# A fourth silu buffer, a reordered unit end, a cast moved by one step and two deferred stores in a fused attention and SwiGLU kernel

## The chip, the cores and the metric

The kernel runs on one core of a Trainium2 chip. The core has five engines with one instruction queue each: TensorE (PE in the profile; its weight loads are shown apart, as PEld), VectorE (DVE), ScalarE (ACT), GpSimd (POOL) and SyncE (SP), which here only issues DMAs. Each engine runs its instructions in the order in which the program issues them and waits on semaphores for the others. The metric is the time of one execution on the device in microseconds; lower is better.

## The reference

Two stages, in float32. Linear attention with a decay per head works on 64-row blocks with a running state `kv_state`; its output, reshaped to 3072 tokens of 512 columns, goes through a SwiGLU block.

```python
# q, k, v: (4, 8, 768, 64); lam: one decay per head
for b in range(nb):
    sl = slice(b * block, (b + 1) * block)
    qb, kb, vb = (q[:, :, sl].copy(), k[:, :, sl].copy(), v[:, :, sl].copy())
    intra = np.einsum('bhic,bhjc->bhij', qb, kb) * Dmask[None]
    intra = np.einsum('bhij,bhjd->bhid', intra, vb)
    inter = np.einsum('bhid,bhde->bhie', qb * lam_pow[None], kv_state)
    out[:, :, sl] = intra + inter
    kb_dec = kb * rev_pow[None]
    kv_state = lam_block[None, :, None, None] * kv_state + np.einsum('bhsd,bhse->bhde', kb_dec, vb)
...
x = np.ascontiguousarray(attn_out.transpose(0, 2, 1, 3)).reshape(B * S, H * D)   # (3072, 512)
g = x @ w_gate                         # w_gate, w_val: (512, 1536)
silu = g * (1.0 / (1.0 + np.exp(-g)))
return (silu * (x @ w_val) @ w_out)    # w_out: (1536, 512)
```

## The kernel before

**Groups and tiles.** The sequence is cut into blocks of 128 rows. A group is two consecutive blocks of one batch element with all 8 heads; there are 12 groups. A tile is two groups, 512 tokens; there are 6 tiles (0 to 5). Attention is done group by group and writes, transposed and in bf16, into the tile's `xt`; the SwiGLU block is done tile by tile. The attention of later groups is woven between the matmuls of earlier tiles.

**Attention of a group.** SP loads k, q and v as float32 (`load_group`). `cast_scaled` (line 285) makes the bf16 tile `qk`: ACT casts k (line 289), DVE, or POOL if so told, scales q (line 291), and then `dma_transpose` (line 276) lets SP issue one transposing DMA into `qkt`. `v_scale` (line 263) makes `v_s` on POOL. On PE follow `scores` (lines 358 or 388; DVE masks them into `ssb`, lines 365 or 393), `upd_mm` (line 420, the update of the state; ACT copies it out, as `kvn` at line 434 and `ups` at line 442, and POOL sums it up in `state`), and the two halves of the output in one pair of banks: `intra` (line 527, from `ssb` and `v_s`) and `inter` (line 514, from `qkt` and the state). Between those two, `guard` (line 498) is a one-column ACT copy out of the output bank; the second half on PE waits for it. `evac` (line 540 or 543) copies the result into `xt`. For group 2, `upd_core` (line 905) issues it in the order: update, first copy, intra, guard, inter, evac, second copy. The queries of groups 0 to 2, which PE transposes, are scaled by the table `qdec` (line 326); the other groups don't read it.

**SwiGLU of tiles 0 to 3.** `ffn_gate` and `ffn_val` (lines 573 and 588) do one 128-column piece of the hidden width: four matmuls for the gate, ACT's silu into a buffer `sil` (line 586), four matmuls for the value, and a DVE product into `h` (line 603). PSUM has eight banks, handed out in turn. Pieces are `steps`; a table `plan`, filled with `at(step, function, ...)`, says what else is issued behind each step, in the order of the `at` calls. Steps of tile 0 are `s0[2]` to `s0[10]`, `s0["11a"]` and `s0["11b"]`; the last two each work on one group.

**SwiGLU of tiles 4 and 5: units.** Here each block product is done with seven block matmuls in place of eight. `ffn_unit` (line 712) is one of three units of a tile. Its operands are sums of blocks of `xt`, of the weights and, for the output, of `h`, made on DVE by `x_combo`, `w_combo` and `h_combo` (lines 710, 692, 666). These sums wait in a list, `trickle`; `drip(n)` issues the next n of them. A unit makes four pairs of silu (ACT, line 756) and product (line 759). The products are on DVE but for the second, which is on POOL. `dr[2]` is the number of sums issued at the unit's end; it is 2 or 3. `mid`, in the first two units of tile 4, issues the first half of the attention of groups 10 and 11.

**Output.** `out_units` (line 801) does the output matmul of tiles 1 to 5 with seven products (line 819), `p1` to `p7`, copies into a buffer `osb`, and stores on SP. For tile 1 it is done in two calls, one per group of the tile; the second call (`t=1, gs=(1,)`) is completed by `out_rest` behind step 9 of tile 2. Its two stores (256 KB each) stand on SP behind the loads of group 9.

**Order on SP around the deferred stores.** Behind step 8 of tile 2: transposition of group 8, loads of group 9. Behind step 9: the two stores. Behind step 0 of tile 3: transposition of group 9, loads of group 10. Behind step 6: transposition of group 10, loads of group 11.

**Buffers.** `sil` has 3 buffers, `h` 5, `osb` 4. A buffer is given out again, in program order, to a later tile of the same tag; the first instruction that writes it waits for the last reader of the one before.

The end of a unit, as it is now:

```python
        for i in range(2):
            product(i, E[i], wa(1, 1), xsum(2))
        silu((1, 0), E[0])
        mult(nc.vector, 1, 0, E[1])
        drip(dr[2])
        if mid:
            mid()
        for i in range(2):
            product(i, Bb[i], wsum(2), xb(1, 1))
        silu((0, 1), Bb[0])
        mult(nc.vector, 0, 1, Bb[1])
        h_combo(t, j)
```

Of the kernel before, what the change touches and what calls it, by code (L numbers as in the profile page):

```python
# [9 lines left out]
BF16 = mybir.dt.bfloat16  # L10
# [27 lines left out]
def _body(ctx, tc, nc, q, k, v, lam, moe_w_gate, moe_w_val, moe_w_out, out):  # L38
    B, H, S, D = q.shape
    HP = H // 2  # L40
# [28 lines left out]
    ssb_pool = ctx.enter_context(tc.tile_pool(name="ssb", bufs=2))  # L69
    xt_pool = ctx.enter_context(tc.tile_pool(name="xt", bufs=2))  # L70
    h_pool = ctx.enter_context(tc.tile_pool(name="h", bufs=5))
    sil_pool = ctx.enter_context(tc.tile_pool(name="sil", bufs=3))
    osb_pool = ctx.enter_context(tc.tile_pool(name="osb", bufs=4))
    kv_pool = ctx.enter_context(tc.tile_pool(name="kv", bufs=1))
    psum = ctx.enter_context(tc.tile_pool(name="psum", bufs=1, space=bass.MemoryType.PSUM))
# [121 lines left out]
    dec = const.tile([128, H, 8], FP32, name="dec")  # L197
    qdn = const.tile([128, H, 2], FP32, name="qdn")
    lamgrp = const.tile([128, HP], FP32, name="lamgrp")
    qdec = const.tile([128, HP, 2, 2 * M], BF16, name="qdec")  # L200
    nc.scalar.activation(ln_lam, lam_ps[:, 0:H], AF.Ln)
    for h2 in range(2):
        nc.scalar.activation(lnp[h2 * 64:h2 * 64 + 64, :],
# [72 lines left out]
    def dma_transpose(g):  # L276
        t = st[("qk", g)]
        tt = qkt_pool.tile([128, 2, 2, HP, 128], BF16, name="qkt", tag="qkt")
        nc.sync.dma_start(out=tt.rearrange("p a s h n -> p (a s h) n"),
                          in_=t.rearrange("p a s x -> p (a s x)"), transpose=True)  # L280
        st[("qkt", g)] = tt

    QP = ()

# [46 lines left out]


    KACT = ()
    later = []

    def run_later(n):
# [314 lines left out]
    def h_combo(t, j, g=None):  # L651


        fs = slice(0, FH) if g is not None else slice(2 * j[0], 2 * j[1]) if type(j) is tuple else slice(2 * j, 2 * j + 2)
        g0, g1 = (0, B // 2) if g is None else (g, g + 1)
        ha, hb = st[("h", t, 0)], st[("h", t, 1)]
        a11, a21 = ha[:, fs, 2 * g0:2 * g1:2], ha[:, fs, 2 * g0 + 1:2 * g1:2]
        a12, a22 = hb[:, fs, 2 * g0:2 * g1:2], hb[:, fs, 2 * g0 + 1:2 * g1:2]
        for i in range(3):
            if ("hs", t, i) not in st:  # L660
                st[("hs", t, i)] = raw_pool.tile([128, FH, B // 2, BLK], BF16, name="hs", tag="raw")
        s = [st[("hs", t, i)][:, fs, g0:g1] for i in range(3)]
        for o, i0, i1, op in ((s[0], a21, a22, ALU.add), (a21, a11, a21, ALU.subtract),
                              (s[1], s[0], a11, ALU.subtract), (s[2], a12, s[1], ALU.subtract)):
            trickle.append((t, lambda o=o, i0=i0, i1=i1, op=op:
                            nc.vector.tensor_tensor(out=o, in0=i0, in1=i1, op=op)))
# [3 lines left out]
    def drip(n):  # L670
        for _ in range(min(n, len(trickle))):
            trickle.pop(0)[1]()
# [39 lines left out]
    def ffn_unit(t, j, bk, early=None, mid=None, dr=(0, 0, 2)):  # L712


        xt = st[("xt", t)]
        for half in range(2):
            if ("h", t, half) not in st:
                st[("h", t, half)] = h_pool.tile([128, FH, B, BLK], BF16, name="h", tag="h")
        hs2 = [st[("h", t, half)][:, 2 * j:2 * j + 2] for half in range(2)]
        A, E, Bb = [[banks[k] for k in bk[2 * m:2 * m + 2]] for m in range(3)]  # L720
        for k in bk:
            primed[k] = 512
        es = [kv_pool.tile([128, 2 * HP * D], FP32, name="es", tag="ups", bufs=4) for _ in range(2)]
        sil = {}

        def product(i, o, lhs, rhs, start=False):
            for fi in range(2):
                for c in range(KH):
                    nc.tensor.matmul(o[:, fi * 256:fi * 256 + 256], lhs(i, c, 2 * j + fi), rhs(c),  # L729
                                     start=(start and fi == 0 and c == 0), stop=(c == KH - 1),  # L730
                                     skip_group_check=True)

        def wa(k, half):
            def f(i, c, fc):
                f0 = (FH * half + fc) * 128
                return (wg_sb, wv_sb)[i][:, KH * k + c, f0:f0 + 128]
            return f

        def wsum(n):
            return lambda i, c, fc: ws[i, n][:, c, fc * 128:fc * 128 + 128]  # L740

        def xb(k, r):
            return lambda c: xt[:, :, KH * k + c, r]

        def xsum(n):
            return lambda c: xs[t][:, n, :, c]

        def h_of(half, r):
            return hs2[half][:, :, r:B:2]

        def v3(x):
            return x.rearrange("p (f g n) -> p f g n", f=2, g=2)

        def silu(key, src):
            sil[key] = sil_pool.tile([128, 512], BF16, name="sil", tag="sil")
            nc.scalar.activation(sil[key], src, AF.Silu)  # L756

        def mult(eng, half, r, src):
            eng.tensor_tensor(out=h_of(half, r), in0=v3(sil[half, r]), in1=v3(src), op=ALU.mult)  # L759

        for i in range(2):
            product(i, A[i], wa(0, 0), xb(0, 0), True)
            nc.scalar.copy(out=Bb[i], in_=A[i])
        for i in range(2):
            product(i, E[i], wa(0, 1), xb(0, 1), True)
            nc.scalar.copy(out=es[i], in_=E[i])
        if early:
            early()
        for i in range(2):
            product(i, Bb[i], wsum(1), xsum(1))  # L770
            nc.vector.tensor_tensor(out=E[i], in0=Bb[i], in1=es[i], op=ALU.add)  # L771
        run_later(len(later))
        drip(dr[0])
        for i in range(2):
            product(i, A[i], wa(1, 0), xb(1, 0))
        silu((0, 0), A[0])
        for i in range(2):
            product(i, Bb[i], wsum(0), xsum(0))
            nc.vector.tensor_tensor(out=es[i], in0=Bb[i], in1=es[i], op=ALU.add)
        mult(nc.vector, 0, 0, A[1])  # L780
        silu((1, 1), es[0])
        mult(nc.gpsimd, 1, 1, es[1])
        drip(dr[1])
        for i in range(2):
            product(i, E[i], wa(1, 1), xsum(2))
        silu((1, 0), E[0])
        mult(nc.vector, 1, 0, E[1])
        drip(dr[2])
        if mid:
            mid()  # L790
        for i in range(2):
            product(i, Bb[i], wsum(2), xb(1, 1))
        silu((0, 1), Bb[0])
        mult(nc.vector, 0, 1, Bb[1])
        h_combo(t, j)

    def out_row(t, b):
# [3 lines left out]
    def out_units(t, gs=(0, 1), last=False, n=7, bk=None, many=None):  # L801
# [20 lines left out]
        def store(g, r, c0, c1, eng=nc.sync if t >= SY else nc.scalar):  # L822
            b = groups[2 * t + g]
            row = b[0] * S + (b[1] * 2 + r) * BLK
            eng.dma_start(out=bass.AP(tensor=out.tensor, offset=out.offset + row * DM + c0,
                                      ap=[[DM, 128], [1, c1 - c0]]), in_=O[g][r][:, c0:c1])

        def p1(g):
            product(A[g], lambda f: ha[:, f, 2 * g], lambda f: wo_sb[:, f, 0:HD], True)
# [203 lines left out]
    def at(n, fn, *a):  # L1033
        plan.setdefault(n, []).append((fn, a))
# [22 lines left out]
    at(s0[9], scores, 2)  # L1057
    at(s0[9], run_later, 4)
    at(s0["11a"], upd_core, 2, SPLIT)
    at(s0[10], cast_scaled, 3, nc.gpsimd)  # L1060
    at(s0[10], load_group, 4, "v")
    at(s0["11b"], v_scale, 3, nc.gpsimd)
    at(s0["11b"], state, 2)
    at(s0["11b"], load_group, 5, "kq")
# [219 lines left out]
```

## Time and profile before

| | us |
|---|---|
| three timed runs: median (lowest to highest) | 218.67 (218.20 to 220.88) |
| profiled execution, its time | 217.92 |
| profiled execution, span from first to last instruction | 216.2 |
| DVE busy in the span | 147.6 |
| ACT busy in the span | 130.6 |

The granted TensorE clock is 1.000 over the whole span. HBM reads are 28.31 MB and writes 6.29 MB.

How rows are read. A timeline row gives the start in us from the span's start, the duration, the engine, the line, the operation, the tile written and the tile read, the shape, and in brackets how long the engine stood idle before it and what it waited for; `x4` is four such instructions in a row, and the duration then is that of all. The suffix q marks an engine's queue where it issues DMAs. A row of waits gives engine, line and tile of who waited, then whom it waited for, the total in us, the number of times and the longest. A row of a tile's view gives shortest, median and longest duration in ns. Matmuls are pipelined, so their rows overlap.

### The profile page before, as it was taken

How to read it: one execution, taken by the hardware profiler on the slowest of the kernel's cores; microseconds unless marked ns; L12 is line 12 of the kernel's file. 1: busy time of each engine (PE TensorE's matmuls, PEld its weight loads, DVE VectorE, ACT ScalarE, POOL GpSimd, SP SyncE). 2: the span in 40 equal slices, each digit the busy share in tenths (PEclk: the TensorE clock that was granted, in tenths of full speed). 3: DMA queues.
4: the chain of work that ended last, by engine and by line, in shares of the span. 5: the costliest groups of instructions: out<-in, count | busy, mean ns of one | idle time of the engine just before them, and what ended most of it. 6: DMA issues, size and time to landing. Idle time of an engine off the chain costs nothing.

```text
span 216.2 us, 6854 instructions
## 1 busy us (share of the span) xinstructions
PE 209.1 (97%) x2797; PEld 153.9 (71%) x2801; DVE 147.6 (68%) x267; ACT 130.6 (60%) x280; POOL 92.1 (43%) x128
## 2 busy tenths in 40 slices
PE   8889999899999999999999999999999999999993
PEld 3566455788888448856754545888888888888882
DVE  1774347576687889765478967887798389961750
ACT  6888576666536154548378587774882676636522
POOL 6685755828499140686953145140730022200200
PEclk9999999999999999999999999999999999999999
DMA  6999999999996788899789859763000500005014
GB/s 193 343 355 382 374 326 293 295 245 232 375 315 137 193 223 199 223 160 256 199 207 222 203 116 212 179 171 126 2 5 3 194 0 3 0 3 194 0 52 147
DMA packets 82177, 39.77 MB, mean 184 GB/s; under 512 B 45410, under 2 KB 77794, under 8 KB 82146
## 3 DMA queue, kind: packets, MB, share of 16 engines
q1 hardware_dynamic: 80946, 38.74, 65.3%
q10 hardware_dynamic: 1200, 0.59, 0.9%
q8 instruction: 22, 0.36, 0.7%
q14 instruction: 9, 0.07, 0.1%
HBM read 28.31 MB, written 6.29 MB: 160 GB/s over the span
## 4 chain that ended last, share of the span: by engine, by line
PE 89%; ACT 3%; DVE 3%; issue 1%; POOLq 1%; POOL 1%; DVEq 0%
PE bank L819 21%; PE bank L581 19%; PE bank L599 19%; PE bank L729 15%; PE bank L619 5%; PE bank L527 2%; PE bank L514 2%; DVE ssb L365 2%; PE bank L420 1%; PE bank L358 1%; PE bank L320 1%; PE bank L388 1%; PE bank L188 1%; ACT sil L756 1%; PE bank L154 1%
## 5 line engine op out<-in xcount | busy, mean ns | idle before, releaser
L603 DVE TENSOR_TENSOR h<-sil,bank 128x256 bf16<-128x256 bf16 (+1 forms) x67 | 35.1, 533 | 29.1 <-PE bank L599 17.6
L581 PE MATMUL bank<-xt,wg_sb 128*128 128x256 bf16 (+1 forms) x276 | 52.6, 315 | 0.0
L599 PE MATMUL bank<-xt,wv_sb 128*128 128x256 bf16 (+1 forms) x276 | 52.4, 314 | 0.0
L586 ACT ACTIVATE sil<-bank 128x256 bf16<-128x256 f32 (+1 forms) x67 | 31.8, 480 | 22.6 <-PE bank L581 17.6
L599 PEld LDWEIGHTS <-wv_sb 128*128 128x128 bf16 x276 | 26.9, 98 | 14.7 <-POOL wv_sb L249 0.2
L581 PEld LDWEIGHTS <-wg_sb 128*128 128x128 bf16 x276 | 26.0, 98 | 13.3 <-DVE xt L540 0.2
L266 POOL TENSOR_TENSOR v_s<-v,dec 128x512 bf16<-128x512 f32 (+1 forms) x18 | 23.2, 1308 | 25.4 <-DMA v<-in_v_dram 21.4
L759 POOL TENSOR_TENSOR h<-sil,es 128x512 bf16<-128x512 bf16 x6 | 7.0, 1167 | 47.9 <-ACT sil L756 47.9
L819 PEld LDWEIGHTS <-h 128*128 128x128 bf16 x240 | 23.3, 98 | 3.6 <-issue 0.6
L819 PE MATMUL bank<-wo_sb,h 128*128 128x256 bf16 x180 | 21.6, 273 | 0.1
L819 PEld LDWEIGHTS <-hs 128*128 128x128 bf16 x180 | 17.6, 98 | 2.7
L365 DVE TENSOR_TENSOR ssb<-bank,causal 128x512 bf16<-128x512 f32 x24 | 15.4, 683 | 2.0 <-PE bank L358 2.0
L729 PEld LDWEIGHTS <-ws 128*128 128x128 bf16 x144 | 13.8, 97 | 2.3 <-issue 0.2
L475 POOL TENSOR_TENSOR kvf<-kvs,ups 128x256 f32<-128x256 f32 x8 | 6.5, 815 | 20.5 <-ACT ups L442 20.5
L771 DVE TENSOR_TENSOR bank<-bank,es 128x512 f32<-128x512 f32 x12 | 7.8, 693 | 10.8 <-PE bank L729 9.4
L819 PE MATMUL bank<-wt,hs 128*128 128x256 bf16 x120 | 15.0, 272 | 0.0
L756 ACT ACTIVATE sil<-bank 128x512 bf16<-128x512 f32 x18 | 10.7, 596 | 7.0 <-POOL h L759 4.7
L759 DVE TENSOR_TENSOR h<-sil,bank 128x512 bf16<-128x512 bf16 x18 | 12.3, 683 | 1.5 <-ACT sil L756 1.4
L729 PE MATMUL bank<-xs,ws 128*128 128x256 bf16 x96 | 12.8, 272 | 0.0
L475 POOL TENSOR_TENSOR kvf<-kvf,ups 128x256 f32<-128x256 f32 x16 | 12.2, 764 | 0.9
L729 PE MATMUL bank<-xt,wg_sb 128*128 128x256 bf16 x72 | 10.8, 273 | 0.2 <-ACT ups L442 0.2
L619 PE MATMUL bank<-wo_sb,h 128*128 128x512 bf16 x45 | 10.7, 379 | 0.2
(119 smaller groups left out, 360.5 us busy)
## 6 DMA issues: line engine op xcount, KB each, us to landing
out_dram<-osb SPq DMA_DIRECT2D x22, 256.0 KB, 2.6
v<-in_v_dram SPq DMA_DIRECT2D x18, 256.0 KB, 4.7
woraw<-in_moe_w_out_dram SPq DMA_DIRECT2D x6, 512.0 KB, 8.2
kraw<-in_k_dram SPq DMA_DIRECT2D x24, 128.0 KB, 3.3
qraw<-in_q_dram SPq DMA_DIRECT2D x24, 128.0 KB, 3.6
wraw<-in_moe_w_gate_dram SPq DMA_DIRECT2D x5, 512.0 KB, 6.9
wraw<-in_moe_w_val_dram SPq DMA_DIRECT2D x5, 512.0 KB, 7.0
kraw<-in_k_dram SPq DMA_DIRECT2D x4, 512.0 KB, 6.7
```

Source lines behind the costliest of these rows:

```text
L266: eng.tensor_tensor(out=st[("vs", g)][:, h0:h1], in0=st[("v", g)][:, h0:h1].rearrange("p h (s d) -> p h s d", s=2), in1=vfac(g, h0, h1), o ...
L365: nc.vector.tensor_tensor(out=ssb[:, h2, 2 * c:2 * c + 2].rearrange("p a s n -> p a (s n)"), in0=sp[(c, h2)].rearrange("p (a x) -> p a x", ...
L475: nc.gpsimd.tensor_tensor(out=o, in0=f, in1=u, op=ALU.add)
L581: nc.tensor.matmul(gp[:, n0:n1], wg_sb[:, mc, fs], xt[:, g0:g1, mc].rearrange("p g b n -> p g (b n)"), start=(mc == 0 and n0 == 0), stop=( ...
L586: nc.scalar.activation(sil[:, 0:N], gp[:, 0:N], AF.Silu)
L599: nc.tensor.matmul(vp[:, n0:n1], wv_sb[:, mc, fs], xt[:, g0:g1, mc].rearrange("p g b n -> p g (b n)"), start=(mc == 0 and n0 == 0), stop=( ...
L603: nc.vector.tensor_tensor(out=h_sb[:, fc % FH, b0:b1].rearrange("p b n -> p (b n)"), in0=sil[:, 0:N], in1=vp[:, 0:N], op=ALU.mult)
L619: nc.tensor.matmul(ps, st[("h", t, fc // FH)][:, fc % FH, b], wo_sb[:, fc, c0:c1], start=(fc == 0), stop=(fc == FC - 1))
L729: nc.tensor.matmul(o[:, fi * 256:fi * 256 + 256], lhs(i, c, 2 * j + fi), rhs(c), start=(start and fi == 0 and c == 0), stop=(c == KH - 1), ...
L756: nc.scalar.activation(sil[key], src, AF.Silu)
L759: eng.tensor_tensor(out=h_of(half, r), in0=v3(sil[half, r]), in1=v3(src), op=ALU.mult)
L819: nc.tensor.matmul(o, lhs(f), rhs(f), start=(start and f == 0), stop=(f == FH - 1), skip_group_check=True)
```

## The change

Five edits. The silu tag gets a fourth buffer. The table `qdec` leaves the constants and takes one of the five `h` buffers. In a unit, the sums of `drip(dr[2])` are issued behind the unit's last product instead of ahead of its last matmuls. The cast of group 3, with its transposition, and the load of group 4's v move from behind step 10 of tile 0 to behind step 11a, where they follow `upd_core` of group 2. The two stores of the second group of tile 1 are not issued where they are written; they are kept in `held` and issued in `dma_transpose(10)`, behind the transposing DMA.

```diff
-    sil_pool = ctx.enter_context(tc.tile_pool(name="sil", bufs=3))
+    sil_pool = ctx.enter_context(tc.tile_pool(name="sil", bufs=4))
...
-    qdec = const.tile([128, HP, 2, 2 * M], BF16, name="qdec")
+    qdec = h_pool.tile([128, HP, 2, 2 * M], BF16, name="qdec", tag="h")
...
         st[("qkt", g)] = tt
+        for put in held.pop(g, []):
+            put()
...
+    HOLD = {(1, 1): 10}
+    held = {}
...
         silu((1, 0), E[0])
         mult(nc.vector, 1, 0, E[1])
-        drip(dr[2])
         if mid:
             mid()
         for i in range(2):
             product(i, Bb[i], wsum(2), xb(1, 1))
         silu((0, 1), Bb[0])
         mult(nc.vector, 0, 1, Bb[1])
+        drip(dr[2])
         h_combo(t, j)
...
         def store(g, r, c0, c1, eng=nc.sync if t >= SY else nc.scalar):
...
-            eng.dma_start(out=bass.AP(tensor=out.tensor, offset=out.offset + row * DM + c0,
-                                      ap=[[DM, 128], [1, c1 - c0]]), in_=O[g][r][:, c0:c1])
+            def put():
+                eng.dma_start(out=bass.AP(tensor=out.tensor, offset=out.offset + row * DM + c0,
+                                          ap=[[DM, 128], [1, c1 - c0]]), in_=O[g][r][:, c0:c1])
+            held.setdefault(HOLD[t, g], []).append(put) if (t, g) in HOLD else put()
...
     at(s0["11a"], upd_core, 2, SPLIT)
-    at(s0[10], cast_scaled, 3, nc.gpsimd)
-    at(s0[10], load_group, 4, "v")
+    at(s0["11a"], cast_scaled, 3, nc.gpsimd)
+    at(s0["11a"], load_group, 4, "v")
     at(s0["11b"], v_scale, 3, nc.gpsimd)
```

## The prediction

> **What bounds the kernel now.** I read the page first: busy times, the chain that ended last, the DMA line.
>
> ```profile
> PE 209.1 (97%) x2797; PEld 153.9 (71%) x2801; DVE 147.6 (68%) x267; ACT 130.6 (60%) x280; POOL 92.1 (43%) x128
> DMA packets 82177, 39.77 MB, mean 184 GB/s; under 512 B 45410, under 2 KB 77794, under 8 KB 82146
> PE 89%; ACT 3%; DVE 3%; issue 1%; POOLq 1%; POOL 1%; DVEq 0%
> ```
>
> TensorE (PE) is busy for 209.1 us of the span of 216.2, it fills 89% of the chain, and the change removes no matmul. All it can give back is PE idle time, 216.2 - 209.1 = 7.1 us, and of that only what lies in the stages it touches. So I looked for PE stalls beside the edits, in the view of waits:
>
> ```profile
> PE bank L729 <- ACT ups L442: 0.2, 1, 0.2
> ACT sil L756 <- POOL h L759: 4.7, 6, 0.8
> ```
>
> PE stands 0.2 us for ScalarE's (ACT's) `ups` copies between two units; its longest wait for ACT, for the guard in group 2's attention, has its own row below. The second line is ACT idle time, up to 0.8 us in front of one silu of each of the six units, because GpSimd (POOL) still holds a buffer; it counts only where PE waits for what ACT does next.
>
> **Group 3's cast behind group 2's attention.** The timeline around the first stall:
>
> ```profile
> 37.12 1.04 ACT L289 CAST qk<-kraw 128x1024 bf16<-128x1024 f32 x1 [0.87 <-DMA kraw<-in_k_dram]
> 37.51 0.66 PE L527 MATMUL bank<-ssb,v_s 64*64 64x128 bf16 x32
> 38.07 0.38 ACT L586 ACTIVATE sil<-bank 128x256 bf16<-128x256 f32 x1
> 38.35 0.36 ACT L434 CAST kvn<-bank 128x256 bf16<-128x256 f32 x1
> 38.60 0.17 ACT L498 COPY guard<-bank 128x1 f32<-128x1 f32 x1
> 38.70 1.92 POOL L291 TENSOR_TENSOR qk<-qraw,dec 128x1024 bf16<-128x1024 f32 x1 [1.58 <-DMA qraw<-in_q_dram]
> 38.83 0.41 PE L514 MATMUL bank<-qkt,kvn 64*64 64x128 bf16 x8 [0.65 <-ACT guard L498]
> 39.27 0.73 ACT L540 CAST xt<-bank 128x512 bf16<-128x512 f32 x1 [0.50 <-PE bank L514]
> 39.87 0.65 ACT L442 COPY ups<-bank 128x256 f32<-128x256 f32 x2
> 40.65 2.96 SPq L279 DMA_TRANSPOSE qkt<-qk  x1
> ```
>
> PE's intra products end at 37.51 + 0.66 = 38.17, the guard is due then, but ACT is inside the cast (37.12 to 38.16, after 0.87 us of waiting for `kraw`), and silu, `kvn` and guard queue behind it. With the cast gone, silu and `kvn` (0.38 + 0.36) fit in front of 38.17; the guard runs to 38.17 + 0.17, and PE goes on 0.06 after it, as at 38.83: at 38.40. Gain 0.4 us, bounds 0.2 and 0.6 (the whole wait).
>
> The 1.04 us cast now runs after the `xt` cast and the copies, which come 0.4 earlier too: from 39.47 + 0.65 = 40.1 to 41.15. Behind it on ACT stand the silus of the next steps, a microsecond late; PE has eight banks, so that nobody on PE is next before ACT has caught up (a half step gives ACT one silu of 0.38, PE eight matmuls): nothing. If that cover were gone, PE would lose the microsecond. POOL's half of the cast keeps its place, since nothing of group 2's attention is on POOL, and ends at 40.62. So the transposition on SP goes out at 41.2 instead of 40.65, 0.55 later; behind it on SP stand the loads of group 4's v and group 5's k and q. Who waits for those:
>
> ```profile
> 43.66 0.56 SPq L115 DMA_DIRECT2D v<-in_v_dram  x1
> 47.13 0.64 PE L358 MATMUL bank<-qkt 64*64 64x128 bf16 x32
> 48.49 1.91 POOL L266 TENSOR_TENSOR v_s<-v,dec 128x1024 bf16<-128x1024 f32 x1 [4.17 <-DMA v<-in_v_dram]
> 50.78 0.22 PE L420 MATMUL bank<-v_s,qk 64*64 64x64 bf16 x2
> L279 SPq DMA_TRANSPOSE qkt<-qk x9: 1597/2234/8702, 40.6 to 141.9; - x9
> DMA to landing us min/median/max: 3.7/4.3/5.5
> ```
>
> The transposition lands at worst at 41.2 + 5.5 = 46.7, just as PE, 0.4 early, wants it for the scores (47.13 - 0.4): nothing. The v load is tight: POOL waits 4.17 us for it and has `v_s` ready at 48.49 + 1.91 = 50.40, PE takes it at 50.78. A PE that is 0.4 early arrives at 50.38, so about 0.1 goes back here even if the load does not move. Does it move by the 0.55? The nine transposition issues last from 1.60 to 8.70 us (median 2.23), and this one, with group 4's q load issued just ahead, 2.96: I read the spread as an issue that ends when the traffic ahead has drained, so that starting it later only shortens it, and v leaves at 43.66 as before. Net of this edit: 0.3.
>
> The Trainium skill ("DMA: Bandwidth & Descriptors", section Rules for kernel authors) says the opposite: a transposition next to ordinary DMAs needs nothing. By it the sum of this edit would be -0.2 instead of +0.3, and the spread of the issue times in the row above speaks against it; it is the first rival.
>
> **Two stores behind group 10's transposition.** They leave their place on SP ahead of transposition 9 and stand behind transposition 10, ahead of group 11's loads.
>
> ```profile
> 112.18 1.34 SPq L825 DMA_DIRECT2D out_dram<-osb  x2
> 115.80 2.23 SPq L279 DMA_TRANSPOSE qkt<-qk  x1
> 127.24 1.23 DVE L291 TENSOR_TENSOR qk<-qraw,qdn 128x1024 bf16<-128x1024 f32 x1 [0.58 <-DMA qraw<-in_q_dram]
> 128.61 1.66 SPq L279 DMA_TRANSPOSE qkt<-qk  x1
> 132.42 0.22 PE L388 MATMUL bank<-qkt 64*64 64x64 bf16 x2
> 139.54 1.22 DVE L291 TENSOR_TENSOR qk<-qraw,qdn 128x1024 bf16<-128x1024 f32 x1
> 140.83 1.04 ACT L289 CAST qk<-kraw 128x1024 bf16<-128x1024 f32 x1
> 141.90 1.60 SPq L279 DMA_TRANSPOSE qkt<-qk  x1
> 146.00 0.45 PE L388 MATMUL bank<-qkt 64*64 64x64 bf16 x32
> ```
>
> Transposition 10 lands at the earliest at 128.61 + 3.7 = 132.31, and PE's scores of group 10 start at 132.42: no slack. The 0.3 us from group 2 could not pass here by itself. Without the stores ahead, transposition 9 should issue like its quiet neighbour (1.66 for 2.23), the loads behind it come 0.57 sooner, VectorE's (DVE's) scaling loses its wait of 0.58, and transposition 10 and its scores can be 0.57 earlier. So this edit gives no time itself; it lets the 0.3 through.
>
> Its price falls on group 11: 1.34 us of issue ahead of its loads, less the 0.57, makes 0.8 us; if the two tiles of 128 x 512 floats, 0.52 MB, cost a full 2.85 us (at the mean 184 GB/s), 2.3. DVE scales q at 139.54, which ends at 140.76, but the transposition at 141.90 waits for ACT's cast, which ends at 141.87: 1.1 us of cover, and from 141.90 + 3.7 = 145.6 to the scores at 146.00 another 0.4. I take 0.8, by the issue row, which is hidden; 2.3 is the slower rival.
>
> **Fourth silu buffer, last product ahead of the sums.** Unit 0 of tile 4, and the ends of two later units:
>
> ```profile
> 150.70 1.35 DVE L759 TENSOR_TENSOR h<-sil,bank 128x512 bf16<-128x512 bf16 x2
> 150.92 1.17 POOL L759 TENSOR_TENSOR h<-sil,es 128x512 bf16<-128x512 bf16 x1 [8.04 <-ACT sil L756]
> 151.97 0.42 DVE L692 TENSOR_TENSOR wg_sb<-wg_sb 128x512 bf16<-128x512 bf16 x1
> 152.13 0.60 ACT L756 ACTIVATE sil<-bank 128x512 bf16<-128x512 f32 x1 [0.75 <-POOL h L759]
> 152.62 0.86 ACT L442 COPY ups<-bank 128x512 f32<-128x512 f32 x2
> 152.97 0.68 DVE L759 TENSOR_TENSOR h<-sil,bank 128x512 bf16<-128x512 bf16 x1
> 153.25 0.31 PEld L729 LDWEIGHTS <-wg_sb 128*128 128x128 bf16 x3 [0.35 <-issue]
> 179.05 0.31 PEld L729 LDWEIGHTS <-ws 128*128 128x128 bf16 x3 [0.18 <-issue]
> 203.96 0.78 ACT L830 COPY bank<-bank 128x256 f32<-128x256 f32 x2
> 204.39 1.62 PEld L819 LDWEIGHTS <-h 128*128 128x128 bf16 x15 [0.27 <-issue]
> ```
>
> The fourth silu of a unit starts when POOL's product ends (150.92 + 1.17 = 152.09, silu at 152.13). Its bank must be written by then too, but the wait is put down to POOL alone. With a fourth buffer it follows the third silu: 0.75 us earlier, and so do the copies behind it on ACT. Three PE gaps hang on those: 0.35 (the `ups` copies free the banks PE wants at 153.25), 0.18 at 179.05, and 0.27 at 204.39, where PE waits for the bank that ACT copies at 203.96 behind the late silu. Each is shorter than 0.75, so all go: 0.8. Gaps under 0.1 at other unit ends I estimate, from the same delay, at 0.1 in all. What is late next is the matmuls themselves.
>
> The new order on DVE: the last product (0.68) would now wait behind two or three sums (152.97 is 0.92 after 152.05) although its silu is ready, so the buffer alone would move it little; put first, it goes out at 152.05, and two or three sums of 0.42 come 0.68 later each, which the emptied slot takes up, since DVE does the same work in all. Readers of these sums are the next unit or output stage, microseconds on: nothing. If they were late, PE would stand up to 0.68 per unit.
>
> Moving `qdec` into the `h` pool costs nothing: its last readers are group 2's multiplications, and until then the five buffers hold only it and tile 0's two halves.
>
> **Sum.** 0.3 + 0.8 + 0.1 = 1.2 us. The profiled execution took 217.92 us (216.2 and 1.7 around it), so 216.7 on its scale. The median of the runs is 218.67, 0.75 above it; on that scale 217.5, which I forecast. With the terms' bounds (0.2 to 0.6 less 0.1 to 0.3; 0.5 to 0.9) the gain is 0.5 to 1.5: 217.2 to 218.2, or 216.4 to 217.4 on the profiled scale.
>
> **Rivals.**
> - The transposition's delay is passed on whole (the rule above). Then v lands 0.55 late, `v_s` is ready at 50.95, PE stands there and is 0.2 behind the old time. For it: POOL starts at 48.49 only on v's landing. Left: 0.9 - 0.2 = 0.7, 218.0. Chance 0.16.
> - The change does not do what it says: the fourth silu still gets the buffer that POOL holds, or ACT is held by something else at once. Then the 0.9 falls away, leaving 0.3 or nothing: 218.4 to 218.7. For it: the three buffers did not rotate in order either, since the silu waits for the second product's buffer, not the first's, which DVE frees. Against: with four buffers, one has been idle since the last unit. Chance 0.12.
> - Slower: the stores hold up group 11. From 1.5 us of delay on (1.1 and 0.4 of cover) PE stands at 146.00. With 2.3 us q is there at 141.84, scaled at 143.06, transposed 4.3 later at 147.4, or 5.5 later at 148.6: PE loses 1.4 to 2.6, keeps the 0.8 behind it: 0.6 to 1.8 slower, 219.3 to 220.5. For it: this stretch's loads are small rows and queue behind the stores; against: DVE waits for no DMA at 139.54, so q was there before. Chance 0.10.
>
> **The numbers.** My forecast gets 0.62, 0.16 and 0.12 go to smaller gains, 0.10 to slower. The range 216.4 to 219.3 takes the forecast on both scales, the first two rivals and the near end of the third. A measurement of this kernel can tell about 2%, 4.4 us, from no change. No case gains 4.4: it would take over half of all PE idle time, most of it in the start and the last store: 0.02. No case loses 4.4 either; for a stall that I do not see, 0.05. Within 2%: 0.93.
>
> **What would show it.** Right: PE's wait for the guard at 0.3 or less; no wait of ACT's silus for POOL in the units; DVE's last product directly behind the third; the PE gaps of 0.35, 0.18 and 0.27 gone; transposition 9 issued in about 1.7 us. Wrong: PE standing at `v_s` of group 4, at the scores of groups 10 or 11, or a unit's first products waiting for DVE sums.

## The result and the profile after

| | before | after |
|---|---|---|
| median (lowest to highest) of 6 runs each, us | 218.82 (218.19 to 220.88) | 216.31 (216.15 to 216.96) |
| ratio of the times | | 0.9891, 95% interval 0.9856 to 0.9926 |
| profiled execution, us | 217.92 | 216.66 |

The change makes the kernel 1.1% faster (0.7 to 1.4%). The two profiled executions differ by 217.92 - 216.66 = 1.26 us, close to the forecast's 1.2; the medians differ by 2.5 us, twice that. The sections below are about that second half.

The page of the changed kernel, busy times and chain of waits (the first row answers to PE's 209.1 us of before, the second to PE's 89%):

```profile
PE 208.1 (97%) x2797; PEld 153.3 (71%) x2801; DVE 148.3 (69%) x267; ACT 130.9 (61%) x280; POOL 92.7 (43%) x128
PE 93%; DMA 2%; DVE 1%; SPq 1%; ACT 0%; issue 0%; DVEq 0%
```

ACT's share of the chain went from 3% to 0%. The line numbers are 2 to 6 higher than before: 498 is now 502, 514 is 518, 692 is 696, 729 is 733, 759 is 763.

Timeline of the changed kernel around the guard of group 2, the transposition of group 3 and the v load behind it:

```profile
37.79 0.67 PE L531 MATMUL bank<-ssb,v_s 64*64 64x128 bf16 x32
38.52 0.16 ACT L502 COPY guard<-bank 128x1 f32<-128x1 f32 x1
38.73 0.41 PE L518 MATMUL bank<-qkt,kvn 64*64 64x128 bf16 x8 [0.28 <-ACT guard L502]
40.29 1.07 ACT L291 CAST qk<-kraw 128x1024 bf16<-128x1024 f32 x1
41.44 2.42 SPq L279 DMA_TRANSPOSE qkt<-qk  x1
43.92 0.56 SPq L115 DMA_DIRECT2D v<-in_v_dram  x1
48.75 1.91 POOL L266 TENSOR_TENSOR v_s<-v,dec 128x1024 bf16<-128x1024 f32 x1 [4.67 <-DMA v<-in_v_dram]
```

PE waits 0.28 us for the guard, where it waited 0.65. The transposition starts 0.79 later than before (41.44 for 40.65) and is issued in 2.42 us instead of 2.96, so the v load leaves 0.26 later. This execution as a whole was 0.28 later from its start-up on (intra at 37.79 for 37.51), so relative to PE the load has not moved.

SyncE's queue in the changed kernel, at the transpositions of groups 9 and 10 and the two stores:

```profile
115.92 1.63 SPq L279 DMA_TRANSPOSE qkt<-qk  x1
...
128.06 1.67 SPq L279 DMA_TRANSPOSE qkt<-qk  x1
129.78 1.08 SPq L830 DMA_DIRECT2D out_dram<-osb  x2
130.90 2.73 SPq L130 DMA_DIRECT2D kraw<-in_k_dram  x4
```

Transposition 9 is issued in 1.63 us for 2.23. And the end of unit 0 of tile 4, on the three engines that matter:

```profile
150.93 1.95 DVE L763 TENSOR_TENSOR h<-sil,bank 128x512 bf16<-128x512 bf16 x3
151.16 1.16 POOL L763 TENSOR_TENSOR h<-sil,es 128x512 bf16<-128x512 bf16 x1 [7.92 <-ACT sil L760]
151.50 0.61 ACT L760 ACTIVATE sil<-bank 128x512 bf16<-128x512 f32 x1
152.12 0.86 ACT L446 COPY ups<-bank 128x512 f32<-128x512 f32 x2
152.78 0.73 POOL L479 TENSOR_TENSOR kvf<-kvs,ups 128x256 f32<-128x256 f32 x1 [0.46 <-ACT ups L446]
152.80 0.99 DVE L696 TENSOR_TENSOR wg_sb<-wg_sb 128x512 bf16<-128x512 bf16 x1
153.14 0.60 PE L733 MATMUL bank<-xt,wg_sb 128*128 128x256 bf16 x4
```

The fourth silu starts at 151.50, while POOL's product still runs (to 152.32). DVE's last product follows its neighbours without a break (x3), the sums come behind it, and PE's 0.35 at this place is gone.

### The profile page after: what moved, and what is told of

The parts are those of the page before. It is cut to its first block, busy times and chain, and to the rows that moved or that the text cites. A ratio compares the mean times of both kernels' runs of the same rounds, so it can differ in the third digit from the quotient of the medians.

```text
span 215.0 us, 6856 instructions
## 1 busy us (share of the span) xinstructions
PE 208.1 (97%) x2797; PEld 153.3 (71%) x2801; DVE 148.3 (69%) x267; ACT 130.9 (61%) x280; POOL 92.7 (43%) x128
## 4 chain that ended last, share of the span: by engine, by line
PE 93%; DMA 2%; DVE 1%; SPq 1%; ACT 0%; issue 0%; DVEq 0%
PE bank L823 22%; PE bank L585 20%; PE bank L603 19%; PE bank L733 17%; PE bank L623 5%; PE bank L531 3%; DMA kraw<-in_k_dram 2%; PE bank L518 2%; PE bank L424 2%; PE bank L362 1%; DVE ssb L369 1%; SPq L115 1%; PE bank L392 1%; PE bank L322 1%; ACT qk L306 0%
## 5 line engine op out<-in xcount | busy, mean ns | idle before, releaser
L479 POOL TENSOR_TENSOR kvf<-kvf,ups 128x256 f32<-128x256 f32 x16 | 13.0, 815 | 0.9
L763 DVE TENSOR_TENSOR h<-sil,bank 128x512 bf16<-128x512 bf16 x18 | 11.8, 683 | 0.3 <-ACT sil L760 0.3
```

Of the source, the lines that this page charges most:

```text
L479: nc.gpsimd.tensor_tensor(out=o, in0=f, in1=u, op=ALU.add)
```

## The experiments

Each kernel is the changed one with the edit shown, unless it says otherwise; ratios are against the kernel before, timed beside it on the same chip (medians of before between 218.18 and 218.72). Two stretches of the trace are used as rulers. **Units**: from PE's first scores matmul of group 11 to its first matmul of the last block product of tile 5, in the changed kernel these two (timeline and the group of line 823):

```profile
146.24 0.45 PE L392 MATMUL bank<-qkt 64*64 64x64 bf16 x32
...
L823 PE MATMUL bank<-wt,hs x24: 269/272/273, 206.2 to 208.8; 128*128 128x256 bf16 x24
```

**Scores**: from the first scores matmul of group 9 to that of group 10. The times in the tables are taken from the trace to 0.01 us. A third stretch, the **end**, goes from where units ends to the end of the span (in the changed kernel 215.0 - 206.2 = 8.8).

### Where are the other 1.2 us: both kernels again, and the change without one or two of its parts

The expectations below set three theories side by side. A: runs of before are late because group 3's k arrives late, ahead of the guard. B: because nothing is left to give at the scores of group 10, so that every late load behind the two stores is paid there. C: the terms of the forecast, and nothing else.

`before_again`: the kernel before, unchanged.

> The kernel before once more, for a second profile and as a control of the ratio (1.000 within 0.003). Theory A: where its time is near 218.8, ACT's cast of group 3 waits more than 0.87 us for k and PE's gap at the guard is above 0.65. Theory B: PE stands at the scores of group 10. Theory C: the same PE gaps as in the first profile, with the start later.

`undo_hold`: the stores at their old place.

```diff
-    HOLD = {(1, 1): 10}
+    HOLD = {}
```

> The changed kernel with the two stores back in their old place. Theory A: no change to 0.3, 216.3 to 216.6, with PE waiting at most 0.3 us at the scores of group 10. Theory B: the lateness of the loads of group 10 reaches PE: 217.5 or more, and the profile shows PE standing at the scores of group 10. Theory C: 216.5 to 216.6.

`undo_cast`: the cast and the load back at their old place.

```diff
-    at(s0["11a"], cast_scaled, 3, nc.gpsimd)
-    at(s0["11a"], load_group, 4, "v")
+    at(s0[10], cast_scaled, 3, nc.gpsimd)
+    at(s0[10], load_group, 4, "v")
```

> The changed kernel with group 3's cast and the load of group 4's v back behind step 10. The timed runs gained 2.5 us where the two profiles differ by 1.3. Theory A (late loads): in most executions the loads of the first 40 us land later than in the profile of before; ACT's cast waits for group 3's k ahead of the guard and hands that lateness to PE, so that moving the cast is worth 1.5 us and more: this kernel takes 217.7 or more. Theory B (scores of group 10 have no slack, and the stores decide): moving the cast is worth 0.2 to 0.4: 216.5 to 216.7. Theory C (the terms as forecast, the rest is that before's profile was one of its fastest executions): also 216.5 to 216.7. The profile: the guard's PE gap back at 0.6 or more.

`units_only`: both of these edits, so that only the fourth buffer and the order in the units are left of the change.

> Before with the silu buffer, the moved table and the new order at a unit's end, but without the cast's move and without the deferred stores. Forecast for these: 0.9 us, so 217.9 against 218.8. Theory A and B: 217.9, the rest is in the two edits left out. Theory C: nearer to the changed kernel, 216.9 to 217.2, since little else has a price.

| | ratio (95% interval) | median; lowest, us | scores stretch, us | PE at the scores of group 10 waits for its transposition, us | end, us |
|---|---|---|---|---|---|
| before, first profile | | | 9.92 | none | 9.21 |
| before_again | 0.9994 (0.9964 to 1.0024) | 218.36; 217.66 | 11.53 | 1.1 | 9.19 |
| undo_hold | 0.9938 (0.9913 to 0.9962) | 217.19; 216.62 | 10.64 | 0.5 | 9.19 |
| units_only | 0.9963 (0.9928 to 0.9998) | 217.95; 216.75 | 9.92 | none | 9.20 |
| undo_cast | 0.9942 (0.9913 to 0.9971) | 216.81; 216.31 | 10.44 | 0.3 | 8.78 |
| after, first profile | 0.9891 (0.9856 to 0.9926) | 216.31; 216.15 | 9.92 | none | 8.79 |

The second profile of the unchanged kernel shows what the first, at 217.92 one of its shorter executions, did not. Its waits of PE, the SyncE queue and DVE's scaling of group 10's q:

```profile
PE bank L388 <- DMA qkt<-qk: 1.1, 1, 1.1
...
PE bank L514 <- ACT guard L498: 0.3, 1, 0.3
```

```profile
113.33 3.29 SPq L825 DMA_DIRECT2D out_dram<-osb  x2
116.78 2.91 SPq L279 DMA_TRANSPOSE qkt<-qk  x1
...
129.47 1.23 DVE L291 TENSOR_TENSOR qk<-qraw,qdn 128x1024 bf16<-128x1024 f32 x1 [2.10 <-DMA qraw<-in_q_dram]
```

Read from below: PE waits 1.1 us for transposition 10; DVE could scale only at 129.47, after 2.10 us of waiting for q; the loads of group 10 went out late because transposition 9 took 2.91 us to issue; and that stood behind the stores. Counted from the scores of group 9, q landed 1.63 us later than in the first profile: 0.39 because transposition 9 started later, just behind the stores' own issue, 0.68 because it was issued longer, and 0.56 because the load itself took longer. Theory B names a real loss. Theory A does not: in this execution, 2.3 us longer than the first, the guard's wait is only 0.3. `undo_hold` shows the same chain on the changed kernel; its median, 217.19, lies between what A and B forecast (216.3 to 216.6, and 217.5 or more):

```profile
112.90 2.85 SPq L830 DMA_DIRECT2D out_dram<-osb  x2
115.92 2.71 SPq L279 DMA_TRANSPOSE qkt<-qk  x1
...
127.79 1.23 DVE L293 TENSOR_TENSOR qk<-qraw,qdn 128x1024 bf16<-128x1024 f32 x1 [1.30 <-DMA qraw<-in_q_dram]
```

`undo_cast` also waits at the scores of group 10 although its stores are moved and its transposition 9 is issued in 1.62 us; there q itself landed late, 5.3 us behind its issue. So the stores are one cause of a late q, not the only one. The guard's wait, forecast to be back at 0.6 or more, was 0.28 there. Its profile has a second loss, far from its edit: q of group 7, for which DVE waits 3.34 us while PE waits for a sum behind it in DVE's queue:

```profile
91.66 1.23 DVE L293 TENSOR_TENSOR qk<-qraw,qdn 128x1024 bf16<-128x1024 f32 x1 [3.34 <-DMA qraw<-in_q_dram]
...
94.00 0.42 DVE L850 TENSOR_TENSOR bank<-bank,osb 128x256 f32<-128x256 f32 x1
```

Five of its twelve runs lie between 217.6 and 218.7 and the other seven between 216.3 and 216.9, where the changed kernel's are. Whether the cast's place has a part in those late loads is open; in the short runs it is worth 0.2 us at most. `units_only` came out at 217.95 as theories A and B had it; its profile, 217.43, is one of its shorter runs and waits at the guard (0.64), not at group 10.

None of the three theories has what the last column shows. The end takes 9.19 to 9.21 us in all five traces with the stores at their old place (the fifth is `only_cast` below), and 8.71 to 8.79 in the nine with the stores elsewhere: 0.4 to 0.5 us less in each of these traces, whatever the loads did. Up to the last copy the end is the same: behind it, the span goes on for 3.08 us before and 2.66 in the changed kernel. The traces have 212 SyncE instructions in the five, 210 in seven of the nine, and 208 in `stores_act` and `hold_both`, the two with 8.71; so the gain goes with what stands on SyncE's queue, but by what mechanism is not shown. So of the 0.9 us between `undo_hold` and the changed kernel (ratios 0.9938 and 0.9891 or 0.9899) not quite half has nothing to do with late loads. The shortest runs, in which little is late, differ so too: 216.62 and 216.75 with the old place in the table above, 216.31 and 216.15 without.

### The cast alone, and the stores at other places

`only_cast`: the kernel before, with the cast and the load moved and nothing else.

> The kernel before, with the cast of group 3 and the load of group 4's v behind group 2's attention and nothing else of the change. Theory A: its 0.4 us pass, 218.1 to 218.3 where the kernel before has 218.6. Theory B: the scores of group 10 wait for a transposition that the stores hold up, which doesn't start earlier because PE does, and so the 0.4 us end there: PE's wait for group 10's transposition is longer by as much, and the time is 218.5 to 218.8.

`stores_ahead_10`: the two stores just ahead of transposition 10 instead of behind it.

```diff
         st[("qkt", g)] = tt
-        for put in held.pop(g, []):
-            put()
```

and the same two lines ahead of the transposing DMA.

> The changed kernel with the two stores kept until group 10, but issued ahead of its transposition instead of behind it. Theory A (what is issued just ahead of a transposition is drained before the transposition is done, and the scores of group 10 have no slack): the transposition lands 1.0 to 1.5 us later, PE stands 0.5 to 1.2 us at the scores of group 10, 0.5 to 1.2 us slower than its neighbour. Theory B (a transposition beside ordinary DMAs needs nothing, the two stores only cost their issue of 0.4 to 0.6 us): at most 0.3 us slower, no wait at the scores above 0.3.

`stores_act`: the old place in the program, on ScalarE's queue.

```diff
-    HOLD = {(1, 1): 10}
+    HOLD = {}
...
+            eng = nc.scalar if (t, g) == (1, 1) else eng
```

> The changed kernel, but the two stores of tile 1 are issued at their old place, ahead of transposition 9, on ScalarE's queue in place of SyncE's. Theory A (traffic): transposition 9's issue lasts until the stores' data has landed, whoever issued them, so it takes 2.2 us or more, q of group 10 lands 4 us or more behind its issue, PE stands 0.4 us or more at the scores of group 10, and the time is 217.0 to 217.4. Theory B (place on SyncE): only the stores' own issue on SyncE was in the way; transposition 9 issues in 1.7 us, PE doesn't stand, 216.2 to 216.7. What the two issues cost ScalarE is not known: by the stores' issues on SyncE 1.3 to 3.3 us, which would show as late silus near 113 us.

`hold_both`: the stores of the tile's first group held back as well, so that four stand behind transposition 10.

```diff
-    HOLD = {(1, 1): 10}
+    HOLD = {(1, 0): 10, (1, 1): 10}
```

> The changed kernel, with the two stores of tile 1's first group held back to transposition 10 as well, so that four stores stand ahead of group 11's loads. Theory A: in the changed kernel PE waits for no transposition at groups 9 and 10 any more, so nothing is left to gain and four stores at group 11 are still covered: 216.2 to 216.8. Theory B: the first two stores too delay the loads of group 9, and without them some runs get shorter: 215.8 to 216.2. Theory C: 2.2 to 2.7 us of issue ahead of group 11's loads pass the cover of 1.5 us, and PE stands at the scores of group 11: 217 or more.

| | ratio (95% interval) | lowest, us | scores stretch, us | transposition 9: issue, us |
|---|---|---|---|---|
| only_cast | 0.9987 (0.9963 to 1.0012) | 217.67 | 10.90 | 2.72 |
| stores_ahead_10 | 0.9924 (0.9891 to 0.9956) | 216.35 | 9.92 | 1.62 |
| stores_act | 0.9902 (0.9868 to 0.9937) | 216.16 | 10.22 | 1.63 |
| hold_both | 0.9913 (0.9883 to 0.9942) | 216.34 | 9.93 | 1.66 |

`only_cast` cannot be told from the kernel before. Its times do not decide between the theories: its median, 218.15, lies where A had it, and its interval takes in no change as well as A's 0.4 us. Its profile, of a run of 219.03, speaks for B: the guard's wait is down to 0.28, and PE waits again at the scores of group 10.

```profile
PE bank L388 <- DMA qkt<-qk: 0.7, 1, 0.7
```

`stores_ahead_10` shows no wait at the scores of group 10, a miss for the theory that stores ahead of any transposition cost half a microsecond. But this profile is of the shortest of its ten runs, 216.35; the median is 216.87 (216.64 in the changed kernel beside it), so a loss in longer runs is not ruled out. In the profiled run SyncE's queue says why there is none:

```profile
122.31 1.02 SPq L130 DMA_DIRECT2D v<-in_v_dram  x2
123.37 2.82 SPq L830 DMA_DIRECT2D out_dram<-osb  x2
127.84 1.66 SPq L281 DMA_TRANSPOSE qkt<-qk  x1
```

The stores landed at 129.28, and the transposition, ready only at 127.84, would have been issued until 129.50 anyhow. Ahead of transposition 9 the room is smaller: there the stores landed between 118.2 and 119.8 in five executions, and its issue ended within 0.3 us of that each time. So what lengthens the issue is traffic that is still in flight. The order on the queue costs too: in three of the five (`before_again`, `undo_hold`, `only_cast`) the stores' own issue ended only 0.2 us ahead of transposition 9, which then started 0.3 to 0.4 us later against the scores of group 9 than in the other two.

`stores_act` did not separate queue from traffic, since it moved the traffic too: on ScalarE's queue the stores had no loads in front of them and left at 107.1 instead of 112 to 114. The second landed at 113.55 (the trace has no landing of the first), and transposition 9 at 116.93 was issued in 1.63 us. Their issue took 0.37 us each on ScalarE. `hold_both` found its cover: with 2.13 us of store issue ahead of group 11's loads, DVE waited 0.58 us for q and PE nothing; at 216.69 it came out as theory A had it. None of the three is faster than the change.

### The units: buffer and order, one at a time

`after_again` is the changed kernel.

> The changed kernel once more, as the control for its neighbours here: ratio to before 0.987 to 0.993, and a profile with no PE wait at the scores of group 10 and no wait of the units' silus for POOL.

It came out so.

`undo_sil`: three silu buffers, sums behind the last product.

```diff
-    sil_pool = ctx.enter_context(tc.tile_pool(name="sil", bufs=4))
+    sil_pool = ctx.enter_context(tc.tile_pool(name="sil", bufs=3))
```

> The changed kernel with three silu buffers, the sums still behind the last product. Theory A (PE's gaps in the units hang on ACT, which waits for POOL at the fourth silu): the gaps of 0.35, 0.18 and 0.27 come back, 0.8 to 1.0 us slower than its neighbour, and ACT waits for POOL 4.7 us in all again. Theory B (the new order on DVE makes the gain by itself): 0.3 us or less slower.

`undo_order`: four buffers, sums ahead of the last matmuls.

```diff
         mult(nc.vector, 1, 0, E[1])
+        drip(dr[2])
...
         mult(nc.vector, 0, 1, Bb[1])
-        drip(dr[2])
```

> The changed kernel with the sums ahead of a unit's last matmuls again, four silu buffers. Theory A: ACT keeps its lead, the PE gaps stay away: 0 to 0.2 us slower than its neighbour; the last product on DVE is 0.9 us later in the first unit and nobody on PE is there for it. Theory B: the gaps come back, 0.5 us or more slower.

| silu buffers | sums | kernel | units stretch, us | ratio (95% interval) | lowest, us |
|---|---|---|---|---|---|
| 3 | ahead | before; before_again; only_cast | 61.00; 60.98; 60.98 | | |
| 4 | ahead | undo_order | 60.88 | 0.9946 (0.9916 to 0.9975) | 217.12 |
| 3 | behind | undo_sil | 61.79 | 1.0009 (0.9975 to 1.0043) | 217.84 |
| 4 | behind | after; after_again | 59.93; 59.93 | 0.9899 (0.9865 to 0.9933), after_again | 216.20 |

This stretch has no loads in its way and repeats to 0.02 us, so it can be read far below what the times of whole runs tell. The buffer alone gives 0.1 us, the order alone costs 0.8, both together give 1.06. Neither is a small term beside the other; they need each other. `undo_sil` was forecast to lose 0.8 to 1.0 and lost 61.79 - 59.93 = 1.86. As theory A had it, PE's gaps of 0.35, 0.18 and 0.27 came back, and ACT waits for POOL 4.6 us in all. But there are new gaps too, the longest of 0.54 (read, like those three, from the weight loads; the matmul row below has 0.36). DVE and PE around that one:

```profile
182.07 0.69 DVE L763 TENSOR_TENSOR h<-sil,bank 128x512 bf16<-128x512 bf16 x1 [0.70 <-ACT sil L760]
182.68 0.42 DVE L670 TENSOR_TENSOR hs<-hs,h 128x512 bf16<-128x512 bf16 x1
...
184.27 1.29 DVE L775 TENSOR_TENSOR bank<-bank,es 128x512 f32<-128x512 f32 x2
```

```profile
185.02 1.20 PE L733 MATMUL bank<-xs,ws 128*128 128x256 bf16 x8 [0.36 <-DVE bank L775]
```

The product now stands first in DVE's queue and waits 0.70 us for the silu that still has no buffer; the sums, which used to fill that time, come behind it, and the next unit's first addition (line 775) is late for PE. With three buffers the old order was the right one.

`undo_order` loses 0.95 us where theory A allowed 0.2. The size is B's, but the gaps of before do not come back; 0.67 of it is one new stall of PE in unit 0, 0.51 of which the row of its matmuls shows. DVE, POOL, ACT and PE there:

```profile
152.11 0.42 DVE L696 TENSOR_TENSOR wg_sb<-wg_sb 128x512 bf16<-128x512 bf16 x1
152.44 0.42 DVE L696 TENSOR_TENSOR wv_sb<-wv_sb 128x512 bf16<-128x512 bf16 x1
152.69 0.76 POOL L479 TENSOR_TENSOR kvf<-kvs,ups 128x256 f32<-128x256 f32 x1 [0.46 <-ACT ups L446]
152.78 0.95 DVE L670 TENSOR_TENSOR h<-h 128x512 bf16<-128x512 bf16 x1
153.65 0.67 DVE L763 TENSOR_TENSOR h<-sil,bank 128x512 bf16<-128x512 bf16 x1
154.41 0.57 ACT L767 COPY bank<-bank 128x512 f32<-128x512 f32 x1 [0.69 <-DVE h L763]
155.03 0.60 PE L733 MATMUL bank<-xs,ws 128*128 128x256 bf16 x4 [0.51 <-ACT bank L767]
```

The third sum lasts 0.95 us where its neighbours of the same size last 0.42: it began 0.09 after POOL's addition to the state and ended 0.28 after it. The fourth buffer lets ACT, and so POOL, go earlier, into the sums; before, POOL's addition came at 153.28, when they were done. Counted from the scores of group 11, the product comes 0.54 us later than in the kernel before (153.65 - 146.15 = 7.50 for 152.97 - 146.00 = 6.97, to rounding), ACT's copy waits 0.69 for it and PE 0.51 for the copy. The collision's 0.95 - 0.42 = 0.53 would account for that wait. To tell this collision from the mere number of sums ahead of the product, the last kernel, `one_behind`, leaves only the last sum behind it:

```diff
         mult(nc.vector, 1, 0, E[1])
+        drip(dr[2] - 1)
...
         mult(nc.vector, 0, 1, Bb[1])
-        drip(dr[2])
+        drip(1)
```

> The changed kernel, with the unit's sums ahead of its last matmuls again, but for the last of the two or three, which stays behind the last product. Theory A (collision): with all sums ahead, it is the third one that costs, since it starts beside GpSimd's addition to the state and lasts 0.95 us for 0.42; behind the product it delays nobody, the product goes out about 0.9 us earlier, at 152.8, the PE gap of 0.67 us in unit 0 of tile 4 is gone whole, and the time is 216.2 to 216.7. Theory B (mere order): each sum ahead of the product costs its 0.34 us of DVE, so that two of them still cost two thirds of what three did: a PE gap of 0.3 us or more stays in unit 0, and the time is 216.9 to 217.3.

```profile
153.40 0.42 DVE L696 TENSOR_TENSOR wv_sb<-wv_sb 128x512 bf16<-128x512 bf16 x1
153.64 0.76 POOL L479 TENSOR_TENSOR kvf<-kvs,ups 128x256 f32<-128x256 f32 x1 [0.45 <-ACT ups L446]
153.73 0.68 DVE L763 TENSOR_TENSOR h<-sil,bank 128x512 bf16<-128x512 bf16 x1
154.33 0.42 DVE L670 TENSOR_TENSOR h<-h 128x512 bf16<-128x512 bf16 x1
```

Two sums still stand ahead of the product, and yet the stall is gone whole; the units stretch is 59.83, the shortest of all. (The other 0.28 of what `undo_order` lost, smaller pieces in later units, is gone as well; no collision was traced there.) (This execution is 0.95 us later here, so 153.73 is 152.78 on the scale of `undo_order`: 0.87 earlier than there.) The product begins beside the same POOL addition and lasts its usual 0.68: it reads one operand from PSUM, where the sum reads both from SBUF. Theory A is right on the mechanism. On the time it missed: 216.84, ratio 0.9927 (0.9899 to 0.9954), lowest 216.20. The profiled execution of it lost 1.2 us elsewhere, behind a late q of group 9:

```profile
PE bank L824 <- DVE bank L851: 1.2, 1, 1.2
```

```profile
103.34 1.68 DVE L293 TENSOR_TENSOR qk<-qraw,qdn 128x1024 bf16<-128x1024 f32 x1 [1.30 <-DMA qraw<-in_q_dram]
```

Five of its ten runs are at 216.2 to 216.5 and five at 217.2 to 217.9. So its 0.1 us in the units cannot be seen in the times, and whether the longer runs all have this stall was not looked at.

## Why the prediction was right, and where it was not

**The sum on the profiled scale came out, in part by luck:** 1.2 forecast, 1.26 measured. By stage, the two profiled executions differ otherwise than the terms. Up to the scores of group 11 the changed kernel is 0.24 us later (146.24 for 146.00): it started 0.28 later, gained 0.37 at the guard, and lost 0.20 between the scores of groups 3 and 4 and 0.12 between those of groups 10 and 11, stretches that differ from execution to execution. The units gave 1.07. The end gave 0.42, for which the forecast has no term; it made up for the cast's 0.3, which did not come through.

**The step to the median failed.** The forecast took the median's 0.75 us above the profiled execution as an offset that both kernels share, and took the same 1.2 off. But the median of before, 218.82, is 0.90 above its profiled execution, and that of the changed kernel, 216.31, is 0.35 below its own; the two together are the other half. The offset of before was a part of what the change removes: waits that the profiled execution happened not to have. So 216.31 lies well below the 217.5 that was forecast for the median (217.2 to 218.2), and 0.1 below the wide range from 216.4. The bounds of the terms add up to a gain of 0.4 to 1.4 (0.2 - 0.3 + 0.5 and 0.6 - 0.1 + 0.9), not 0.5 to 1.5.

- **Cast, 0.3 forecast.** The guard's wait fell by 0.37 between the two profiles (0.65 to 0.28), as worked out. But the longer wait is in only two of the four traces with the cast at its old place, 0.65 in before and 0.64 in `units_only`, where ACT's cast itself waited 0.87 and 0.85 for k; in `before_again` and `undo_cast` k came in time, and the wait was 0.28 already. Nothing went back at `v_s` of group 4: ready at 48.75 + 1.91 = 50.66, PE did not wait there. In `units_only`, with the cast at its old place, PE did wait 0.5 there for a late v; that load varies by itself.
- **Stores, "gives no time itself".** This is the term that was mis-sized, at nothing for about 0.9 us by the ratios of `undo_hold` and the changed kernel (with intervals that overlap). Of that, 0.41 is the end, which the forecast does not have. Its mechanism was read rightly: transposition 9 issued in 1.63 us (forecast about 1.7), DVE's wait of 0.58 for q gone, no slack at the scores of group 10. The forecast then used the slack as a bar to gains, and not the other way round: with no slack, each late load behind the stores is a loss. By the scores stretch, five executions with the stores at the old place (9.92, 11.53, 10.90, 10.64, 9.92) average 10.58, nine with the stores elsewhere 10.05, so 0.5; with the 0.41 that is the 0.9. That the 0.3 could not pass without it fits the profile of `only_cast`.
- **Price at group 11, 0.8 hidden.** Right: PE waits for nothing there, and not with four stores either.
- **Units, 0.9.** 1.06 measured. The three gaps of 0.35, 0.18 and 0.27 are gone, 0.8 as forecast; the small ones, put at 0.1, gave 0.26. "The buffer alone would move it little" was right (0.1), though the reason given, the product's place behind two or three sums, missed that the third of them collides with POOL. "Nothing" for the readers of the later sums is right with four buffers, and wrong by 0.8 us with three.
- **First rival**, the transposition's delay passed on whole: no. The issue started 0.79 later and took 0.54 less. In both profiles it ended with group 4's q, the load issued just ahead of it: at 43.60 before and 43.86 after, where q landed at 43.74 and 43.94. Five executions show the same at transposition 9: its issue ended at 118.03, 119.69, 118.63, 118.68 and 119.28, and the stores' data had landed at 118.18, 119.83, 118.90, 118.55 and 119.48 (before, before_again, undo_hold, units_only, only_cast). The rule of the Trainium skill that stood behind this rival ("DMA: Bandwidth & Descriptors", section Rules for kernel authors) stands there in a row on transpositions that corrupt each other, and says nothing of time; read as a rule on time, it does not hold here.
- **Second rival**, the silu still gets POOL's buffer: no; ACT waits for POOL in no unit. **Third**, the stores hold up group 11: no.

The account: about 218.7 - 216.4 = 2.3 us. Of it 1.06 lie in the units and 0.41 at the end, in every trace; about 0.5, on the mean, at the scores of group 10 (waits of 0 to 1.1); and 0.37 at the guard in two of four traces, on the mean 0.2. These make about 2.2. The last two differ from run to run and were seen in too few profiles to be split more finely.

## What to carry to other kernels

Where the trace shows a wait of nearly zero in front of the critical engine, behind a chain of DMAs, one profile does not price it: take a second one, a longer execution, before you call an edit there free. An edit that frees a buffer and one that reorders the queue behind it may each be worth nothing, or less, alone; ask of each what it does without the other. When a forecast sum agrees with the measured one, add up the stages of both traces before you believe its terms; here one term was missing and another was eaten up. And a stage without loads in it can be timed in the trace to hundredths of a microsecond, when whole runs cannot tell half a per cent.

## What the runs showed of the hardware

- **The issue of a transposing DMA waits for traffic ahead of it.** At transposition 9 it took 2.23 to 2.91 us in the five executions with the two stores in flight, and ended within 0.3 us of their landing; with the stores elsewhere it took 1.62 to 1.66 in eight executions and 2.01 in after_again, where group 9's v landed at 118.64 and the issue ended at 118.54. Over all 126 transpositions of the 14 traces, 62 were issued in 1.59 to 1.69 us; of the 64 longer ones, 59 ended between 0.42 us ahead of the last landing recorded of what was issued before them and 0.24 behind it. Of the other five, four have DMAs ahead of them whose landing the trace lacks; the fifth, transposition 6 of undo_cast with 3.30 us, has none near it, and what held it is open. This is an inference from pairs of times; the queue itself was not seen.
- **The same load lands after very different times.** Group 10's q landed 4.2 to 4.8 us behind the end of its issue in the five executions with the stores at the old place; of the nine others, 2.7 to 3.3 in six, 4.0 in stores_act and 5.3 in undo_cast, for which no cause was found. The trace of hold_both lacks this landing.
- **A sum on VectorE from two SBUF operands and a GpSimd addition hold each other up.** The sum took 0.95 us for 0.42 in undo_order, 0.99 in the changed kernel, where PE does not wait for it; a product with one operand in PSUM is not held up. The Trainium skill ("SBUF — State Buffer", section Who interferes with whom) says this: a VectorE instruction with two inputs in SBUF contends with a GpSimd instruction that reads SBUF, and whichever is issued first blocks the other. The rows agree, in the order too: GpSimd's addition began 0.09 us ahead in undo_order, 0.02 ahead in the changed kernel. The other order is in before_again, where the sum went first and the addition took 0.92 us for 0.73:

```profile
134.24 0.41 DVE L666 TENSOR_TENSOR hs<-hs,h 128x512 bf16<-128x512 bf16 x1
134.32 0.92 POOL L475 TENSOR_TENSOR kvf<-kvs,ups 128x256 f32<-128x256 f32 x1 [1.49 <-ACT ups L442]
```
